# Attention with top-k and two expert layers: the first pair's preparation, the routing's instructions, the gathers' buffers and the fold table are rearranged

## The chip, the cores and the metric

One NeuronCore of a Trainium2 chip runs the whole program. The metric is the device time of one execution in microseconds (us); lower is better. The core has five engines with a queue of their own each, and they meet only through semaphores: TensorE (PE: matmuls and transposes through the array; its weight loads are listed as PEld), VectorE (DVE), ScalarE (ACT), GpSimd (POOL) and SyncE (SP), whose queue issues most of the DMAs. Matmul results land in PSUM, everything else lies in SBUF or in DRAM.

## What is computed

The reference has three stages, on 4 batches of 576 tokens with 8 heads of 64 columns (so 2304 tokens of 512 columns):

```python
# attention, for each batch and head
scores = scale * (q @ k.T)                                  # 576 x 576
kth = the 32nd largest of each row of scores
scores = where(scores >= kth, scores, -1e9)
attn = softmax(scores)                                      # with 1e-9 added to the sum
x[:, head] = attn @ v
# experts: one of 8 for each token that is not skipped
do_compute = x @ w_skip > 0
e_idx = argmax(x @ w_gate);  gate_w = softmax(x @ w_gate)[e_idx]
x[do_compute] += gate_w * (relu(x @ w1[e_idx]) @ w2[e_idx]) # 512 -> 1024 -> 512
# gated layer for all tokens
g = x @ w_gate2;  out = (g * sigmoid(g) * (x @ w_val)) @ w_out   # 512 -> 1536 -> 512
```

## The kernel before

The tokens are worked on in two groups of two batches (`NG`, `BG`). For each group: attention, routing, experts (`moe1`), gated layer (`moe2`).

**Attention** (`attention`, L333) goes through 16 pairs of heads (group, batch, pair), each with nine tiles of 128 query rows: four of the first head, one that holds the last 64 rows of both heads, four of the second (`SEQ`, L305). For each tile PE makes the scores (`scores`, L200), ACT copies them out (`head`, L212), and DVE finds the 32 largest of each row (`rows_tile`, L225): a maximum of the two halves (`hi`, L222 or L236), then rounds of MAX8 and MATCH_REPLACE8 (L241, L255, L256). POOL makes the minima in the first half (L252, L253) and the bias `nb` of the exponential (L243). In the first half (`whole(w)`: nine pairs) PE and ACT apply the mask; after that DVE does (L260). `trans` and `pv` (L272, L281) transpose the weights and multiply by v. The second step of `pv` (L301) multiplies the result by `fold`, a table for each head with an identity folded in two, the gate's 8 columns and the skip's one: so one product gives the 64 output columns and the head's share of the routing logits.

**Preparation of a pair** (`prep`, L112). q and k are needed with the head's columns on the partitions, and as two fp32r parts whose sum is the fp32 value. For each of the two heads (i) and for k, then q: the rows are loaded, the high part is copied and the low part subtracted into the tile `nat` (L149, one buffer), which `prep_t` (L178) transposes on PE into a bank of `side_bank` (one bank in the first half) and copies out on ACT. For the first pair (`first`) ACT makes the high parts (L154) and DVE the low ones (L160); for all others POOL makes both (L156, L159, L160). All loads are issued by SP. The first pair has nothing beside it; each later pair is prepared during the nine tiles of the one before.

**Routing** (`route`, L454, `first_slots`, L534) runs once for each group and batch, on five tiles of up to 128 tokens. DVE takes the largest of 8 logits, the index of the first that equals it and a one-hot row; PE counts the tokens ahead of each with triangular ones; DVE reads off the rank. `first_slots` then builds, with a one-hot of the rank (`hot`) and a product on PE, the list of the first 128 token rows of each expert, with the gate's weight (`ids`). Loops over the five tiles issue one small instruction for each (L478, L487, L521, L543). L527 to L532 compute a slot in a table of all tokens; only `tables` reads it, inside a branch (`rest`, L738) that runs when an expert has more than 128 tokens of a group or when a row has a tie at the 32nd place.

**Experts** of the first group (`moe1_whole`, L1058) run among the tiles of the second group's attention. For expert e, `gather` (L967) fetches its rows from DRAM into a tile `io` with an indirect DMA on POOL's queue, one expert ahead; `turn` transposes them (L1070); the two layers follow in fp32; DVE adds the gated result into the same tile (L1104), and `scatter` (L975) writes the rows back. `io` has two buffers (`nio`, the last argument of `Moe` at L657). `moe2` of that group uses the same tile to load its rows and to store its output. In between, `split_gated` (L563) converts and splits the gated layer's weights, on DVE (L611 to L613), ACT (L590) and POOL (L591).

**The order of the work.** The Python code writes the instructions in an order that interleaves these stages by counts of steps (`run`, L615; `ORDER`, L30). The tile framework then simulates the program and draws each engine's order from priorities and simulated times (`high_priority`, `issue_after` are hints to it), and puts in the semaphores. On the chip each engine runs its list strictly in that order.

## Time and profile before

| | us |
|---|---|
| median of 3 runs | 1231.78 |
| lowest and highest run | 1224.69, 1232.47 |
| the profiled execution | 1217.23 |
| its span, first to last instruction | 1215.4 |
| PE busy | 1158.9 |
| DVE busy | 976.2 |
| ACT busy | 733.4 |
| POOL busy | 592.2 |

The profile is one execution, with its own time. Times in the rows are microseconds from the first instruction of the span. An instruction counts as busy from its start to its end, waits inside it included; matmul ends are modelled. The entry in brackets at the end of a row is how long the engine was idle before it, and what released it.

### The profile page before, as it was taken

The numbers are of one execution on the slowest core, as the hardware profiler recorded it, in microseconds if no ns is written. First come the engines' busy times: TensorE is split into PE (matmuls) and PEld (weight loads), VectorE is DVE, ScalarE is ACT, GpSimd is POOL, SyncE is SP. The second block draws the span as 40 slices with busy tenths as digits, with TensorE's granted clock in tenths as the row PEclk, the third lists the DMA queues.
The fourth block names the chain that finished last, engine by engine and source line by source line (L and its number), as shares of the span: only waits on it lengthen the run. The fifth ranks groups of instructions, "written<-read, shape, count | busy, mean of one in ns | idle before, by whom it ended". The sixth has DMA issues, their size and how long they took to land.

```text
span 1215.4 us, 21497 instructions
## 1 busy us (share of the span) xinstructions
PE 1158.9 (95%) x7253; PEld 1002.6 (82%) x7254; DVE 976.2 (80%) x2366; ACT 733.4 (60%) x1582; POOL 592.2 (49%) x770
## 2 busy tenths in 40 slices
PE   6999889999899999999999999999999999999997
PEld 5777778777687877888887799899998799898996
DVE  6999999999999999999999982369888268184480
ACT  5989988999664565656555442267767344343440
POOL 6788867888243434335444433222111535555550
PEclk9999999999899999999998999999999999999999
DMA  2023621111178979876655786799888534543430
GB/s 70 22 79 122 204 66 40 39 36 35 62 248 279 322 256 323 293 252 214 210 189 208 258 298 218 267 342 296 293 269 289 189 101 124 171 125 119 150 102 29
DMA packets 136796, 219.11 MB, mean 180 GB/s; under 512 B 37860, under 2 KB 95204, under 8 KB 130404
## 3 DMA queue, kind: packets, MB, share of 16 engines
q1 hardware_dynamic: 129652, 178.86, 44.6%
q0 software_dynamic: 7024, 38.78, 9.3%
q8 instruction: 59, 0.97, 0.3%
q14 instruction: 61, 0.50, 0.1%
HBM read 177.77 MB, written 41.95 MB: 181 GB/s over the span
## 4 chain that ended last, share of the span: by engine, by line
PE 47%; DVE 19%; DMA 8%; issue 3%; ACT 3%; POOL 1%; SPq 0%; DVEq 0%; POOLq 0%; ACTq 0%
PE m L1155 7%; PE m L1156 7%; PE m L1157 7%; DVE tops L256 5%; DVE rest L255 5%; PE m L1179 4%; PE m L1180 4%; PE m L1178 4%; PE m L1101 2%; DVE pp L260 2%; PE pT L291 1%; DVE rest L248 1%; PE pT L277 1%; DMA h2h<-in_moe_w_out_dram 1%; DMA wraw<-in_moe_w_dram 1%
## 5 line engine op out<-in xcount | busy, mean ns | idle before, releaser
L256 DVE MAX8 tops<-rest 128x8 f32<-128x288 f32 (+1 forms) x432 | 229.2, 545 | 1.2
L1155 PE MATMUL m<-x2h,whl 128*128 128x384 f32 x576 | 196.0, 341 | 1.9 <-ACT x2h L1140 1.4
L1157 PE MATMUL m<-x2h,whl 128*128 128x384 f32 x576 | 194.0, 338 | 0.9 <-POOL whl L591 0.9
L1156 PE MATMUL m<-x2l,whl 128*128 128x384 f32 x576 | 194.6, 338 | 0.0
L1124 POOL TENSOR_TENSOR whl<-wfly,whl 128x1024 fp32r<-128x1024 f32 x54 | 129.5, 2399 | 111.6 <-ACT whl L1123 111.6
L1123 ACT ACTIVATE whl<-wfly 128x1024 fp32r<-128x1024 f32 x69 | 73.2, 1060 | 105.2 <-PE m L1157 65.5
L279 ACT ACTIVATE pt<-pT 128x512 f32<-128x512 f32 (+2 forms) x320 | 112.1, 405 | 37.4 <-PE pT L277 36.0
L255 DVE MATCH_REPLACE8 rest<-tops,rest 128x288 f32<-128x288 f32 x288 | 125.7, 437 | 0.0
L218 ACT ACTIVATE sc<-pS 128x576 f32<-128x576 f32 x144 | 93.6, 650 | 32.9 <-PE pS L208 24.9
L277 PE MATMUL pT<-idn,pp 128*128 128x128 f32 (+1 forms) x720 | 109.7, 278 | 3.0 <-DVE pp L260 1.0
L1155 PEld LDWEIGHTS m<-x2h,whl 128*128 128x128 f32 x576 | 108.0, 188 | 5.4 <-ACT x2h L1140 1.7
L1157 PEld LDWEIGHTS m<-x2h,whl 128*128 128x128 f32 x576 | 108.1, 188 | 1.4 <-POOL whl L591 1.3
L208 PE MATMUL pS<-kT,qT 128*128 128x288 f32 x512 | 105.4, 326 | 3.4 <-DVE hi L222 1.6
L1156 PEld LDWEIGHTS m<-x2l,whl 128*128 128x128 f32 x576 | 108.2, 188 | 0.5
L1167 DVE TENSOR_TENSOR h2l<-th,h2h 128x384 fp32r<-128x384 f32 x36 | 86.3, 2397 | 23.9 <-ACT h2h L1166 23.9
L960 DVE TENSOR_TENSOR whl<-wraw,whl 128x1024 fp32r<-128x1024 f32 x64 | 80.4, 1269 | 20.8 <-ACT whl L959 19.1
L1164 DVE SCALAR_TENSOR_TENSOR th<-th,m 128x384 f32<-128x384 f32 x72 | 39.1, 543 | 71.4 <-ACT th L1163 71.4
L243 POOL TENSOR_SCALAR nb<-tops 128x1 f32<-128x1 f32 x144 | 36.8, 255 | 121.9 <-DVE tops L241 101.3
L277 PEld LDWEIGHTS pT<-idn,pp 128*128 128x128 f32 (+1 forms) x720 | 80.7, 137 | 13.1 <-issue 6.4
L208 PEld LDWEIGHTS pS<-kT,qT 128*128 128x128 f32 x512 | 77.9, 196 | 9.9 <-ACT sc L218 2.8
L1178 PE MATMUL m<-whl,h2h 128*128 128x512 f32 x216 | 84.9, 398 | 0.5 <-DMA whl<-w2s 0.3
L1179 PE MATMUL m<-whl,h2h 128*128 128x512 f32 x216 | 85.2, 394 | 0.0
(205 smaller groups left out, 2913.9 us busy)
## 6 DMA issues: line engine op xcount, KB each, us to landing
wfly<-w2s SPq DMA_DIRECT2D x69, 512.0 KB, 3.5
whl<-in_moe_w_dram SPq DMA_DIRECT2D x32, 1024.0 KB, 6.2
wraw<-in_moe_w_dram SPq DMA_DIRECT2D x64, 512.0 KB, 5.4
whl<-w2s POOLq DMA_DIRECT2D x31, 1024.0 KB, 6.3
w2s<-h2h SPq DMA_DIRECT2D x8, 1024.0 KB, 8.8
w2s<-whl SPq DMA_DIRECT2D x8, 1024.0 KB, 9.3
io<-xa SPq DMA_DIRECT2D x18, 256.0 KB, 4.1
out_dram<-io SPq DMA_DIRECT2D x18, 256.0 KB, 2.1
```

Source lines behind the costliest of these rows:

```text
L208: m = self.nc.tensor.matmul(pS[:, x, :W], l, r[:, x * W:(x + 1) * W], start=(n == 0), stop=stop and n == len(ops) - 1)
L218: self.nc.scalar.activation(sc, pS[:, :, :W], AF.Copy, scale=BIG if on_pe else 1.0)
L255: self.mark = nc.vector.match_replace(hj, h[:, (j - 1) * 8:j * 8], hi if j == 1 else hj, NEG)
L256: nc.vector.max(h[:, j * 8:(j + 1) * 8], hj if j < 3 else rest.rearrange("p a b -> p (a b)"))
L277: self.anchor = nc.tensor.transpose(p[:k, c - a, :], pp[:, c * P:c * P + k], self.idn)
L279: nc.scalar.activation(T[:k, a:z, do:do + n], p[:k, :z - a, so:so + n], AF.Copy)
L1124: self.fly_engine.tensor_tensor(lo, raw, hi.bitcast(F32), op=OP.subtract)
L1155: nc.tensor.matmul(pz, wh[:, z, k, :], xh[:, k, :], start=(k == 0), stop=False)
L1156: nc.tensor.matmul(pz, wh[:, z, k, :], xl[:, k, :], start=False, stop=False)
L1157: nc.tensor.matmul(pz, wl[:, z, k, :], xh[:, k, :], start=False, stop=(k == 3))
L1178: nc.tensor.matmul(po[t], hh[:, f, s], wh[:, k, :], start=(f == 0), stop=False)
L1179: nc.tensor.matmul(po[t], hh[:, f, s], wl[:, k, :], start=False, stop=False)
```

## The change

- `fold` has one entry for two heads: the identity stands once, with the even head's nine weight columns ahead of it and the odd head's behind it. `pv` takes the 73 columns that it needs from either side; so an even head's output now stands behind its logits (`finish_pair` reads it there). POOL makes 4 instead of 8 identities, and eight smaller loads replace four.
- First pair, first head only (`lead`): q's two loads of this head go out on ACT's queue; q's `nat` lies in a pool of its own (`tmp`); the transposes go to `pt_bank`, three banks instead of one; DVE takes the copies of k's tail and of q's second half. The first pair's second head is prepared as all others are, on POOL.
- Routing: the loops over five tiles become single instructions over all five (L479, L488, L522, L544). The table of column numbers becomes bf16.
- The slot arithmetic moves into a new function `slots`, called from `tables`, with tiles kept for each group and batch (`routed`).
- `io` of the first group's experts gets three buffers.

```diff
@@ -43 @@
         self.rps = None
-        self.L, self.ids = {}, {}
+        self.L, self.ids, self.routed = {}, {}, {}
         self.const = ctx.enter_context(tc.tile_pool(name="const", bufs=1))
@@ -64 @@
         E, D, H = self.E, self.D, self.H
-        self.fold = c.tile([P, H, D + E + 1], F32, name="fold")
-        for h in range(H):
-            nc.gpsimd.tensor_tensor(self.fold[:, h, :D], self.idn[:, :D], self.idn[:, D:], op=OP.add)
+        M = E + 1
+        self.fold = c.tile([P, H // 2, D + 2 * M], F32, name="fold")
+        for j in range(H // 2):
+            nc.gpsimd.tensor_tensor(self.fold[:, j, M:M + D], self.idn[:, :D], self.idn[:, D:], op=OP.add)
...
         self.before = c.tile([P, P], BF, name="before")
-        self.column = c.tile([P, P], F32, name="column")
+        self.column = c.tile([P, P], BF, name="column")
         nc.gpsimd.iota(self.column, pattern=[[1, P]], base=0, channel_multiplier=0,
@@ -83 @@
                        allow_small_or_imprecise_dtypes=True)
-        self.ebase = c.tile([P, 5, E], F32, name="ebase")
-        nc.gpsimd.iota(self.ebase, pattern=[[0, 5], [self.GT, E]], base=0, channel_multiplier=0,
-                       allow_small_or_imprecise_dtypes=True)
         self.rows = c.tile([P, NT, 1], I32, name="rows")
...
             f = self.fold[x * D:(x + 1) * D]
-            nc.sync.dma_start(f[:, :, D:D + E], self.a["moe_w_gate"].rearrange("(h p) e -> p h e", p=D))
-            nc.sync.dma_start(f[:, :, D + E], self.a["moe_w_skip"].rearrange("(h p) -> p h", p=D))
+            for hh, o in ((0, 0), (1, D + E + 1)):
+                nc.sync.dma_start(f[:, :, o:o + E],
+                                  self.a["moe_w_gate"].rearrange("(h z p) e -> z p h e", z=2, p=D)[hh])
+                nc.sync.dma_start(f[:, :, o + E], self.a["moe_w_skip"].rearrange("(h z p) -> z p h", z=2, p=D)[hh])
         self.nblk = c.tile([1, self.NG * E], I32, name="nblk")
@@ -116 @@
         def load(nm, t, i, parts=(0, 1)):
-            src, eng = self.a[nm], nc.sync
+            src = self.a[nm]
+            eng = nc.scalar if first and i == 0 and nm == "q" else nc.sync
             o = src.offset + (b * self.H + h + i) * S * D
@@ -146 @@
                 n = 5 - i
-                t = sb.tile([P, 5, 3 * D], F32R, name="nat", bufs=1)
+                lead = first and i == 0
+                t = (self.tmp if lead and nm == "q" else sb).tile([P, 5, 3 * D], F32R, name="nat", bufs=1)
                 o = t[:, :n, :w * D].rearrange("p c (t e) -> p c t e", t=w)
                 src = raws[nm][:, i, :n, :]
-                if first:
+                if lead:
                     for z in range(0, w, 2):
@@ -157 @@
                     nc.gpsimd.tensor_scalar(o[:, :, 0, :], src, 1.0, 1.0, op0=OP.mult, op1=OP.mult)
-                (nc.vector if first else nc.gpsimd).tensor_tensor(o[:, :, 1, :], src, o[:, :, 0, :].bitcast(F32),
+                (nc.vector if lead else nc.gpsimd).tensor_tensor(o[:, :, 1, :], src, o[:, :, 0, :].bitcast(F32),
                                                                   op=OP.subtract)
-                nat = (nm, i, t, kT, qT, qt)
+                nat = (nm, i, t, kT, qT, qt, lead)
                 yield
@@ -175 @@
-    def prep_t(self, nm, i, t, kT, qT, qt):
+    def prep_t(self, nm, i, t, kT, qT, qt, lead):
         nc, D = self.nc, self.D
+        bank = self.pt_bank if lead else self.side_bank
+        def copy(o, p, alt):
+            if lead and alt:
+                nc.vector.tensor_copy(o, p)
+            else:
+                nc.scalar.activation(o, p, AF.Copy)
         nz = 1 if nm == "k" else 2
         for z in range(nz):
-            p = self.side_bank(F32R)
+            p = bank(F32R)
             for c in range(4):
                 nc.tensor.transpose(p[:, c, :], t[:, c, D * z:D * z + P], self.idr)
-            nc.scalar.activation(kT[i][:, :512] if nm == "k" else qT[i][:, z, :],
-                                 p.bitcast(F32).rearrange("p c e -> p (c e)"), AF.Copy)
+            copy(kT[i][:, :512] if nm == "k" else qT[i][:, z, :], p.bitcast(F32).rearrange("p c e -> p (c e)"),
+                 nm == "q" and z == 1)
         if i:
             return
-        p = self.side_bank(F32R)
+        p = bank(F32R)
         for z in range(nz):
...
             if nm == "k":
-                nc.scalar.activation(kT[j][:, 512:], pf[:, 0, s], AF.Copy)
+                copy(kT[j][:, 512:], pf[:, 0, s], True)
             else:
@@ -284 @@
         M = D + self.E + 1
+        fold = self.fold[:, h // 2, :M] if h % 2 == 0 else self.fold[:, h // 2, M - D:]
         v = R["v"]
@@ -298 @@
         for j, (so, n, dst) in enumerate(outs):
-            nc.tensor.matmul(p[:n, j, :M], oT[:, so:so + n], self.fold[:, h], start=True, stop=True)
+            nc.tensor.matmul(p[:n, j, :M], oT[:, so:so + n], fold, start=True, stop=True)
         for j, (so, n, dst) in enumerate(outs):
@@ -432 @@
             cols = slice(j * P + hh * D, j * P + (hh + 1) * D)
-            nc.sync.dma_start(d[b * S:b * S + 512, cols].rearrange("(p c) d -> p c d", c=4), x[:, :4, hh, :D])
-            nc.sync.dma_start(d[b * S + 512:(b + 1) * S, cols], x[:64, 4, hh, :D])
+            nc.sync.dma_start(d[b * S:b * S + 512, cols].rearrange("(p c) d -> p c d", c=4), x[:, :4, hh, M - D if hh == 0 else 0:][:, :, :D])
+            nc.sync.dma_start(d[b * S + 512:(b + 1) * S, cols], x[:64, 4, hh, M - D if hh == 0 else 0:][:, :D])
         yield
...
             for hh in range(2):
-                nc.gpsimd.tensor_tensor(l, l, x[:n, s, hh, D:], op=OP.add)
+                nc.gpsimd.tensor_tensor(l, l, x[:n, s, hh, D * hh:][:, :, :M - D], op=OP.add)
         if j == H // 2 - 1:
@@ -467 @@
         nc.vector.tensor_reduce(m, lg, axis=AX.X, op=OP.max)
-        do = t2("do")
+        if (g, b) not in self.routed:
+            self.routed[g, b] = (c.tile([P, NT, E], BF, name=f"oh{g}{b}"), c.tile([P, NT], F32, name=f"sl{g}{b}"),
+                                 c.tile([P, NT], F32, name=f"do{g}{b}"))
+        oh, sl, do = self.routed[g, b]
+        if every:
+            do = t2("do")
         nc.vector.tensor_scalar(do, L[:, :, E], 0.0, None, op0=OP.is_gt)
...
         if every:
-            do = t2("all")
+            do = self.routed[g, b][2]
             nc.vector.memset(do, 1.0)
...
         eq = t3("eq")
-        for t in range(NT):
-            nc.vector.scalar_tensor_tensor(eq[:, t], lg[:, t], m[:, t:t + 1], self.erow[:, t], op0=OP.is_equal,
-                                           op1=OP.mult)
+        def wide(x):
+            return x[:, :, None].to_broadcast([P, NT, E])
+        nc.vector.tensor_tensor(eq, lg, wide(m), op=OP.is_equal)
+        nc.vector.tensor_tensor(eq, eq, self.erow, op=OP.mult)
         d = t3("d")
-        nc.vector.tensor_tensor(d, lg, m[:, :, None].to_broadcast([P, NT, E]), op=OP.subtract)
+        nc.vector.tensor_tensor(d, lg, wide(m), op=OP.subtract)
         nc.scalar.activation(d, d, AF.Exp)
...
         nc.vector.tensor_reduce(idx, eq, axis=AX.X, op=OP.min)
-        oh = t3("oh", BF)
-        for t in range(NT):
-            nc.vector.scalar_tensor_tensor(oh[:, t], self.erow[:, t], idx[:, t:t + 1],
-                                           do[:, t:t + 1].to_broadcast([P, E]), op0=OP.is_equal, op1=OP.mult)
+        nc.vector.tensor_tensor(eq, self.erow, wide(idx), op=OP.is_equal)
+        nc.vector.tensor_tensor(oh, eq, wide(do), op=OP.mult)
         yield
@@ -517 @@
         yield
-        rk, sl = t3("rk"), t2("sl")
-        for t in range(NT):
-            nc.vector.scalar_tensor_tensor(rk[:, t], pk[:, t * E:(t + 1) * E], 1.0, oh[:, t], op0=OP.mult, op1=OP.mult,
-                                           accum_out=sl[:, t:t + 1])
+        rk = t3("rk")
+        nc.vector.tensor_tensor(rk, pk[:, :NT * E].rearrange("p (t e) -> p t e", t=NT), oh, op=OP.mult)
+        nc.vector.tensor_reduce(sl, rk, axis=AX.X, op=OP.add)
         if not every:
...
         nc.vector.tensor_copy(data[:, :, 0:1], rows)
-        ns = t2("ns")
+    def slots(self, g, b):
+        nc, c, NT, E = self.nc, self.const, 5, self.E
+        oh, sl, do = self.routed[g, b]
+        ns = c.tile([P, NT], F32, name="r_ns")
+        rk = c.tile([P, NT, E], F32, name="r_rk")
+        idx = c.tile([P, NT], F32, name="r_idx")
         nc.vector.tensor_scalar(ns, do, -1.0, -1.0e6, op0=OP.add, op1=OP.mult)
@@ -540 @@
         hot = self.at.tile([P, 5, P], F32, name="hot")
-        for t in range(5):
-            nc.vector.tensor_scalar(hot[:, t], self.column, rank[:, t:t + 1], None, op0=OP.is_equal)
+        nc.vector.tensor_tensor(hot, self.column[:, None, :].to_broadcast([P, 5, P]),
+                                rank[:, :, None].to_broadcast([P, 5, P]), op=OP.is_equal)
         yield
@@ -627 @@
             with ExitStack() as s1:
-                tmp = self.pool(s1, "tmp")
+                tmp = self.tmp = self.pool(s1, "tmp")
                 self.at1 = self.pool(s1, "attn1")
@@ -654 @@
                     pass
-            mo = Moe(self, self.pool(st, "moe"), self.psum_pool(st, "pm"), 3, ring, 2)
+            mo = Moe(self, self.pool(st, "moe"), self.psum_pool(st, "pm"), 3, ring, 3)
             mo.ready = ready
@@ -758 @@
         sent = sb.tile([P, n, 2], I32, name="sent")
+        self.ebase = sb.tile([P, 5, self.E], F32, name="ebase")
+        nc.gpsimd.iota(self.ebase, pattern=[[0, 5], [self.GT, self.E]], base=0, channel_multiplier=0,
+                       allow_small_or_imprecise_dtypes=True)
         nc.gpsimd.iota(sent[:, :, 0], pattern=[[0, n]], base=self.GT, channel_multiplier=0)
...
             nc.sync.dma_start(tab.rearrange("(p n) c -> p (n c)", p=P), sent.rearrange("p n c -> p (n c)"))
+            for b in range(self.BG):
+                self.slots(g, b)
             for t in range(self.NT):
...
```

## Rows read from the trace of the kernel before

**Rows 1.** Windows: microseconds busy of each engine in three stretches (start:end, length)

```profile
13.00:315.00 302.00, 282.96 (x2125) 231.19 (x2125) 301.15 (x971) 269.35 (x705) 234.74 (x391) 0.99 0.24 72
315.00:700.00 385.00, 367.15 (x2275) 304.05 (x2274) 372.56 (x999) 218.87 (x511) 159.74 (x226) 0.98 0.71 243
...
760.00:1215.00 455.00, 443.57 (x2483) 407.92 (x2482) 268.00 (x305) 218.31 (x307) 171.27 (x92) 0.99 0.58 191
```

**Rows 2.** Timeline of the start: start, length, engine, line, operation [idle before, releaser]

```profile
1.22 1.22 SPq L130 DMA_DIRECT2D raw<-in_k_dram  x2
...
3.10 1.10 SPq L130 DMA_DIRECT2D raw<-in_q_dram  x2
...
3.89 0.47 ACT L154 ACTIVATE nat<-raw 128x320 fp32r<-128x320 f32 x1 [1.21 <-DMA raw<-in_k_dram]
...
4.98 0.75 PE L184 MATMUL pR<-idr,nat 128*128 128x128 f32 x4 [4.98 <-DVE nat L160]
...
6.41 0.37 PE L191 MATMUL pR<-idr,nat 128*128 128x128 f32 x1 [0.69 <-ACT kT L185]
...
7.04 0.83 ACT L154 ACTIVATE nat<-raw 128x320 fp32r<-128x320 f32 x2
...
7.54 0.49 DVE L160 TENSOR_TENSOR nat<-raw,nat 128x320 fp32r<-128x320 f32 x1 [2.35 <-ACT nat L154]
...
8.87 0.60 ACT L185 ACTIVATE qT<-pR 128x512 fp32r<-128x512 f32 x1 [1.01 <-PE pR L184]
...
11.52 0.85 PE L208 MATMUL pS<-kT,qT 128*128 128x288 f32 x2
...
12.41 0.65 ACT L218 ACTIVATE sc<-pS 128x576 f32<-128x576 f32 x1 [0.94 <-PE pS L208]
...
13.09 0.46 DVE L236 TENSOR_TENSOR hi<-sc 128x288 f32<-128x288 f32 x1 [5.06 <-ACT sc L218]
...
13.14 1.07 POOL L252 TENSOR_TENSOR sm<-sc 128x288 int32<-128x288 int32 x1 [6.38 <-ACT sc L218]
```

**Rows 3.** The tile nat in the first 30 us: durations in ns, min/median/max

```profile
L160 DVE TENSOR_TENSOR nat<-raw,nat x4: 491/529/735, 4.4 to 16.9; 128x320 fp32r<-128x320 f32 x2, 128x256 fp32r<-128x256 f32 x2
...
L160 POOL TENSOR_TENSOR nat<-raw,nat x2: 876/877/878, 23.9 to 28.2; 128x320 fp32r<-128x320 f32 x2
```

**Rows 4.** DVE by lines, 166 to 187 us (one routing): count, us, mean ns, idle

```profile
L488 DVE SCALAR_TENSOR_TENSOR r_oh<-erow,r_idx,r_do 128x8 bf16<-128x8 f32 x5 | 1.3, 314 | 0.0
L544 DVE TENSOR_SCALAR hot<-column,r_sl 128x128 f32<-128x128 f32 x5 | 1.1, 274 | 0.0
...
L479 DVE SCALAR_TENSOR_TENSOR r_eq<-L,r_m,erow 128x8 f32<-128x8 f32 x5 | 0.8, 212 | 0.0
L528 DVE TENSOR_SCALAR r_ns<-r_do 128x5 f32<-128x5 f32 x1 | 0.7, 679 | 0.0
...
L522 DVE SCALAR_TENSOR_TENSOR r_rk<-pR,r_oh 128x8 f32<-128x8 f32 x5 | 0.5, 145 | 0.0
...
L482 DVE TENSOR_TENSOR r_d<-L,r_m 128x40 f32<-128x40 f32 x1 | 0.2, 183 | 0.0
```

**Rows 5.** Timeline behind two of the gathers

```profile
372.15 1.04 POOL L969 DMA_INDIRECT io<-xa,ids  x1 [3.35 <-DMA xa<-io,ids]
...
376.55 0.63 PE L1070 MATMUL m<-idn,io 128*128 128x128 f32 x4 [2.40 <-DMA io<-xa,ids]
...
378.45 0.46 DVE L222 TENSOR_TENSOR hi<-sc,pS 128x288 f32<-128x288 f32 x1 [1.80 <-ACT sc L218]
...
408.04 0.46 DVE L222 TENSOR_TENSOR hi<-sc,pS 128x288 f32<-128x288 f32 x1 [1.06 <-ACT sc L218]
```

**Rows 6.** Waits of POOL's engine over the run: us in total, times, longest

```profile
POOL io L969 <- DMA xa<-io,ids: 10.2, 5, 3.7
```

**Rows 7.** Timeline at 347 us, DVE and POOL

```profile
347.19 2.35 POOL L591 TENSOR_TENSOR h2h<-h2h 128x1024 fp32r<-128x1024 f32 x1
...
347.73 2.43 DVE L260 SCALAR_TENSOR_TENSOR pp<-sc,tops,e 128x576 f32<-128x576 f32 x1
```

## The prediction

> **What bounds the kernel now.** I read the busy time by stretch first, because the averages of the page mix stages with different limits [rows 1]. From 13 to 315 us VectorE (DVE) is busy 301.15 of 302.00 us, while TensorE (PE) has 19 us idle: the first half of the attention is set by DVE, and every DVE microsecond taken out of it moves all that follows. From 315 to 700 us, where attention, the first group's experts and the weight splitting share the core, DVE is busy 372.56 of 385.00 and PE 367.15: DVE still leads, with 12.4 us of idle time, but PE is close behind. From 760 on PE is busy 443.57 of 455.00 and DVE 268.00; there time taken from DVE is worth nothing, and work that starts earlier simply ends earlier.
>
> Then I read the timeline of the start [rows 2]. DVE's first attention instruction starts at 13.09, after 5.06 us idle, and until then the engines take turns on one chain: k is split (ACT, then DVE), transposed (PE), copied out (ACT), and only then q is split, because k and q share one buffer of the tile `nat`, and one PSUM bank. Next come the DVE instructions of one routing [rows 3, 4], and last what the experts' gathers wait for [rows 5, 6].
>
> **The change part by part.**
>
> *First pair side by side.* Both ends of the chain stay; the middle is run in parallel. k is unchanged up to its transposes, which end at 4.98 + 0.75 = 5.73. q's two loads of the first head leave from ACT's queue, which at the start has only the table load and one copy to do; the last piece of q (the second head's 64-row tail) is SP's fourth issue: k's tails are issued by 1.22 + 1.22 = 2.44, one issue costs half of 1.10, so 2.99. k's last tail was issued by 2.44 and ACT took k at 3.89, 1.45 later; so q is there at about 4.45. ACT copies it by 4.45 + 0.83 = 5.28, DVE subtracts by 5.8 (0.49). PE does k's tail by 5.73 + 0.37 = 6.10, q's first half by 6.85 and the second by 7.6 (0.75 each). With three banks no copy blocks them, and the second half's copy goes to DVE, which idles there; the trace has no such copy on DVE, so I take ACT's 0.60 for it and get 8.2. Scores: first half 6.85 + 0.60 + 0.85 = 8.3, second half to 9.15, eviction 0.65: DVE starts at about 9.9 instead of 13.09. A gain of **3.1**. Bounds: if ACT issues the two loads only behind its first copy, q comes some 1.5 later and 1.6 is left; if they also hold back ACT's copy of k (two issues of 0.55), 0.5; 3.6 at best.
>
> *The second head's splits on POOL.* Two DVE subtractions at 529 ns [rows 3] leave the stage that DVE bounds: **1.0** gained. On POOL they cost two at up to 0.88 plus two copies, say 3.0 us. What hides them: POOL idles 6.38 us before its first attention instruction at 13.14 [rows 2], and half of its eight fold additions go as well. If that cover is gone, POOL's part of the first tile is up to 3 us late; DVE then has the next tiles' maxima to do, so the bounds are -1.3 and 1.3.
>
> *Routing on five tiles at once.* Per routing, from one of the four [rows 4]: L488 1.3, L479 0.8, L544 1.1, L522 0.5 and L528 0.7 go, with four small ones behind L528 (0.5 in all, none over L482's 0.18): 4.9 us. In come five instructions of 128x40 and one reduction of the same size, 6 x 0.18 = 1.1, and one comparison of 128x640: from 0.18 at 40 elements and 0.46 at 288 (the first `hi` in rows 2) 1.13 ns each, so 0.18 + 600 x 1.13 ns = 0.86. Net 3.0. Without the stretched rows (L528 at 0.2, L488 at L479's 0.8) it is 2.0. I take 2.5, between them. Three routings lie in the stage that DVE sets (168, 303, 528 us): **7.5**, bounds 6.0 and 9.0. The fourth, at 773, is where PE is the bound: nothing. The slot arithmetic goes into a branch of which the trace shows no instruction.
>
> The merged comparison is the one place where a rule speaks against the edit. The Trainium skill ("VectorE: DVE Perf Modes", section on the TRN2 errata) gives 58 + elements/speed-up cycles, with a speed-up of 2 for an fp32 tensor_scalar out of SBUF and none for tensor_tensor: an estimate by that page is 5 x 122 cycles = 0.64 us before and 698 cycles = 0.73 after, a loss of 0.1 where the rows give a gain of 0.24. By the page the sum would be 1.0 lower.
>
> *Three row blocks.* With two, the gather for expert e+1 must wait until the scatter of e-1 has landed, since it writes into that block. POOL waits 10.2 us for this over five gathers [rows 6], and what stands behind on its queue waits too: at 372.15 the gather starts after 3.35 us idle, the bias `nb` of a softmax tile comes behind it, PE sits 2.40 us before the transposes of the gathered rows, and DVE idles 1.80 until 378.45 [rows 5]. The same ends in 1.06 us at 408.04. With a third block the gather waits for a scatter one expert older, long landed. I count the two that DVE shows: **2.9**, bounds 0 and 8 (most of DVE's 12.4 idle there). What is late next is the scatter's own wait for its expert's result.
>
> *Nothing.* The shared fold table: the multiplication keeps its 73 columns. Its eight loads instead of four add four SP issues, about 2.5 us of SP's queue at 10 to 15 us, ahead of the next pair's loads; the next pair's splits are needed some 30 us later. If that cover failed, it would be up to 2.5.
>
> Sum: 3.1 + 1.0 + 7.5 + 2.9 = 14.5. The profiled execution took 1217.23 us (span 1215.4), so 1202.7 by its measure. The median of the runs shown stands 14.55 higher, at 1231.78; from it, **1217.3**.
>
> **The rivals.**
>
> A. *The second half gives nothing.* PE is 95% busy there, and a stall taken from one engine may only be handed to the next. For it: PE's 367.15 of 385. Against: the gap at 378 runs through both. The third routing and the gathers fall away: 14.5 - 2.5 - 2.9 = 9.1, 1222.7.
>
> B. *The wide instructions are held by POOL.* At 347.73 a DVE instruction with two SBUF inputs takes 2.43 us beside a POOL subtraction of 2.35 that started just before [rows 7]. Five of the new wide instructions have two SBUF inputs, the merged comparison among them, where its five predecessors had one tensor input. If each is held for half of a POOL instruction of 1.07 (the one at 13.14), a routing gains nothing: 5 x 0.5 = 2.5. Then 14.5 - 7.5 = 7.0, 1224.8. Against: the old L488 and L479 had two inputs as well, and more instructions to be caught. The Trainium skill ("SBUF — State Buffer", section "Who interferes with whom") states it as a rule: a VectorE instruction with two SBUF inputs and a GpSimd instruction that reads SBUF exclude each other for a whole instruction. By that rule, the pair at 347 agrees.
>
> C. *The gather's wait moves into PE's queue: slower.* The order on each engine is drawn at build from simulated times. With the third block the transposes of gathered rows may be put earlier among the scores than the data really lands; PE works in order, so scores, and then DVE, wait behind them. Place: L1070, eight experts. Price: DVE idled 1.80 for PE's 2.40, three quarters. Without the gathers' 2.9 the change gains 11.6; it turns into a loss from a wait of 11.6 / 0.75 / 8 = 1.9 us per expert. At POOL's present 3.35 it is 20.1 - 11.6 = 8.5 lost, 1240.3. Against: a gather issued sooner also lands sooner.
>
> D. *The second half closes up.* If all of DVE's 12.4 us idle goes instead of 2.9, the gain is 24.0, 1207.8. For it: the bias behind a waiting POOL is a common end of the gaps there. Against: most of them are shorter than a microsecond and end with other things.
>
> **How the numbers follow.** Chances: my forecast 0.52 (its own range 1211 to 1223, from the bounds of the four terms taken in moderate mixture), A 0.16, B 0.12, D 0.12, C 0.08. The range 1203 to 1229 takes in A, B and D, with D's end stretched by 5 for the spread of the runs (the quickest of before stands 7.1 under the median) and the upper end by the low bounds of all terms; it leaves out C and tails. A measurement of this kernel tells about 1% from no change, here 12.3 us, so faster means under 1219.5: 0.7 of my forecast, D and a little of A, 0.54. Slower is C, 0.07. The rest, 0.39, is within.
>
> **What would show it.** Right: the first `hi` near 10 us; about 2.5 us less DVE time in each routing; L969 no longer waiting for a landing; DVE's busy time down by some 9 to 11 us (the fourth routing included), its stage ending near 685 instead of 700. Wrong: a first `hi` after 11.5; the merged comparison over 1.2 us; new idle time before L1070; or DVE's idle time from 315 on grown by more than the start has won.

## The result, and the profile after

The kernel after takes **1213.74 us** (median of 12 runs, 1209.92 to 1218.01). The kernel before takes 1224.58 in the 12 runs beside it (1216.64 to 1232.47). The ratio is 0.9914, with a 95% interval of 0.9890 to 0.9939: some 10.5 us quicker. 1217.3 was predicted, with a drop of 14.5 us.

The profiled execution after took 1210.6 us, with a span of 1208.7: 6.7 under the span of before, whose profiled execution is one of its quicker ones. Both profiles can be accounted for on PE, which is busy 96% of the span: after, its idle time is 52.1 us against 56.5 of before (1.8 less until 13 us, 0.8 less until 315, 1.1 less until 760, 0.8 less behind it), and its busy time is 2.3 less. No single place gives the gain. The last routing starts at 773.0 before and at 774.0 after, so the 6.7 us lie behind it: PE does 5.9 us less from 760 us on (443.57 and 437.64), as it stood still 3.7 less until then, and its busy time is 2.3 less in all.

The windows of the kernel after, columns as in [rows 1]:

```profile
13.00:315.00 302.00, 283.71 (x2120) 229.00 (x2119) 299.38 (x941) 268.58 (x702) 232.19 (x389) 0.99 0.24 72
315.00:700.00 385.00, 368.24 (x2277) 306.57 (x2275) 365.26 (x947) 217.86 (x503) 162.04 (x225) 0.98 0.75 251
760.00:1208.00 448.00, 437.64 (x2461) 399.89 (x2458) 264.31 (x280) 215.51 (x303) 174.88 (x90) 1.00 0.60 192
```

DVE has lost 7.3 us of work between 315 and 700 us, but has not closed up: it idles 19.7 us there, where it idled 12.4. PE's busy time is 1.1 higher. The attention, which was to end near 685 us, ends *later* than before (the last MAX8 of a `hi` by 6 us); it is the other work of that stretch (the first group's experts, the weight splitting) that is 4 to 10 us earlier.

The start of the kernel after, as in [rows 2]:

```profile
0.77 0.41 ACTq L123 DMA_DIRECT2D raw<-in_q_dram  x1
...
1.22 0.56 ACTq L131 DMA_DIRECT2D raw<-in_q_dram  x1
...
1.80 1.28 ACT L63 ACT_TABLE_LOAD   x1 [1.68 <-issue]
...
4.16 1.45 ACT L156 ACTIVATE nat<-raw 128x320 fp32r<-128x320 f32 x3 [0.75 <-DMA raw<-in_k_dram]
...
5.21 0.75 PE L194 MATMUL pT<-idr,nat 128*128 128x128 f32 x4 [5.21 <-DVE nat L162]
...
7.38 0.69 DVE L186 CAST qT<-pT 128x512 fp32r<-128x512 f32 x1 [0.90 <-PE pT L194]
...
8.00 0.68 PE L218 MATMUL pM<-kT,qT 128*128 128x288 f32 x2
...
8.48 0.67 PE L194 MATMUL pR<-idr,nat 128*128 128x128 f32 x4
...
8.94 0.81 PE L218 MATMUL pS<-kT,qT 128*128 128x288 f32 x2
...
9.79 0.65 ACT L228 ACTIVATE sc<-pS 128x576 f32<-128x576 f32 x1
...
10.47 0.57 DVE L246 TENSOR_TENSOR hi<-sc 128x288 f32<-128x288 f32 x1 [2.40 <-ACT sc L228]
```

The first `hi` starts at 10.47 instead of 13.09: 2.6 us won. ACT's two issues push its table load to 1.80, and the copy of k comes at 4.16 instead of 3.89.

DVE's lines in the first routing of the kernel after, columns as in [rows 4]:

```profile
L566 DVE TENSOR_TENSOR hot<-column,sl 128x640 f32<-128x640 bf16 x1 | 1.3, 1342 | 0.0
...
L487 DVE TENSOR_SCALAR do<-L 128x5 f32<-128x5 f32 x1 | 0.8, 830 | 0.0
...
L499 DVE TENSOR_TENSOR r_eq<-r_eq,erow 128x40 f32<-128x40 f32 x1 | 0.3, 348 | 0.0
...
L506 DVE TENSOR_TENSOR oh<-r_eq,do 128x40 bf16<-128x40 f32 x1 | 0.2, 186 | 0.0
...
L498 DVE TENSOR_TENSOR r_eq<-L,r_m 128x40 f32<-128x40 f32 x1 | 0.2, 180 | 0.0
```

The new wide instructions take 0.18 to 0.35 us here (up to 0.54 in the second routing), the merged comparison 1.34 here and about 0.8 in the other three. With every DVE instruction of a routing counted from the end of the one before it, the four routings took 6.67, 6.88, 5.23 and 5.16 us before, and take 3.87, 3.05, 2.84 and 3.23 after. The merged comparison of 1.34 starts just behind an instruction on POOL:

```profile
183.03 0.79 POOL L263 TENSOR_TENSOR rest<-sm,hi 128x288 int32<-128x288 int32 x1 [1.54 <-DVE tops L266]
183.17 1.34 DVE L566 TENSOR_TENSOR hot<-column,sl 128x640 f32<-128x640 bf16 x1
```

The gathers (L997) and scatters (L1004) of the first group in the kernel after, on POOL's timeline, and POOL's wait for them over the run, against [rows 5, 6]:

```profile
323.78 1.89 POOL L997 DMA_INDIRECT io<-xa,ids  x1 [1.40 <-DVE rest L265]
325.96 0.97 POOL L997 DMA_INDIRECT io<-xa,ids  x1 [0.30 <-issue]
327.24 0.95 POOL L997 DMA_INDIRECT io<-xa,ids  x1 [0.30 <-issue]
361.23 1.08 POOL L1004 DMA_INDIRECT xa<-io,ids  x1 [7.62 <-DVE io L1132]
367.78 1.17 POOL L997 DMA_INDIRECT io<-xa,ids  x1 [5.47 <-DMA xa<-io,ids]
```

```profile
POOL io L997 <- DMA xa<-io,ids: 15.9, 4, 5.5
```

Three gathers are issued ahead instead of two, so no PE instruction waits for gathered rows any more (three waited 3.9 us before). But four of the five later gathers still come right behind the scatter that frees their block, and POOL still waits for that landing: 15.9 us, where it was 10.2.

### The profile page after: what moved, and what is told of

The parts are those of the page before. It is cut to its first block, busy times and chain, and to the rows that moved or that the text cites. A ratio compares the mean times of both kernels' runs of the same rounds, so it can differ in the third digit from the quotient of the medians.

```text
span 1208.7 us, 21428 instructions
## 1 busy us (share of the span) xinstructions
PE 1156.7 (96%) x7253; PEld 997.0 (82%) x7254; DVE 969.1 (80%) x2275; ACT 731.2 (60%) x1576; POOL 600.7 (50%) x769
## 4 chain that ended last, share of the span: by engine, by line
PE 46%; DMA 10%; DVE 10%; ACT 3%; issue 2%; POOL 1%; SPq 0%; DVEq 0%; ACTq 0%; POOLq 0%
PE m L1183 6%; PE m L1184 6%; PE m L1185 6%; PE m L1207 4%; PE m L1208 4%; PE m L1206 4%; DMA wraw<-in_moe_w_dram 4%; PE m L1116 3%; DVE whl L988 2%; DMA w2s<-h2h 2%; PE m L1129 2%; PE pT L302 2%; PE pS L218 2%; PE pT L287 2%; DVE tops L266 1%
## 5 line engine op out<-in xcount | busy, mean ns | idle before, releaser
L287 PE MATMUL pT<-idn,pp 128*128 128x128 f32 (+1 forms) x720 | 113.2, 278 | 0.3 <-DVE pp L270 0.3
L218 PE MATMUL pS<-kT,qT 128*128 128x288 f32 x512 | 101.8, 321 | 4.9 <-DVE hi L232 2.7
L987 ACT ACTIVATE whl<-wraw 128x1024 fp32r<-128x1024 f32 x64 | 67.2, 1061 | 33.1 <-DMA wraw<-in_moe_w_dram 24.4
L1206 PE MATMUL m<-whl,h2h 128*128 128x512 f32 x216 | 85.9, 401 | 0.6 <-DVE x2l L1169 0.6
L1195 POOL TENSOR_TENSOR h2l<-th,h2h 128x384 fp32r<-128x384 f32 x36 | 46.2, 1283 | 80.7 <-ACT h2h L1194 80.6
```

Of the source, the lines that this page charges most:

```text
L218: m = self.nc.tensor.matmul(pS[:, x, :W], l, r[:, x * W:(x + 1) * W], start=(n == 0), stop=stop and n == len(ops) - 1)
L287: self.anchor = nc.tensor.transpose(p[:k, c - a, :], pp[:, c * P:c * P + k], self.idn)
L1195: lo_engine.tensor_tensor(hl[:, f, :], th, hh[:, f, :].bitcast(F32), op=OP.subtract)
L1206: nc.tensor.matmul(po[t], hh[:, f, s], wh[:, k, :], start=(f == 0), stop=False)
```

## The experiments

The change has three parts that can be made alone, so these came first, with the kernel before run again as its own control.

**lead_only**: the first pair side by side (with the second head's splits on POOL), nothing else.

```diff
-            src, eng = self.a[nm], nc.sync
+            eng = nc.scalar if first and i == 0 and nm == "q" else nc.sync
...
-                t = sb.tile([P, 5, 3 * D], F32R, name="nat", bufs=1)
+                t = (self.tmp if lead and nm == "q" else sb).tile([P, 5, 3 * D], F32R, name="nat", bufs=1)
...
-                (nc.vector if first else nc.gpsimd).tensor_tensor(o[:, :, 1, :], src,
+                (nc.vector if lead else nc.gpsimd).tensor_tensor(o[:, :, 1, :], src,
...
-            p = self.side_bank(F32R)
+            p = bank(F32R)
```

> Only the first pair is changed: q's loads on ACT's queue, its own nat tile, three banks, two copies on DVE, and the second head's splits on POOL; routing, row blocks and fold table as before. If my terms stand and add, the first hi is at 10.5 us as in the changed kernel and the run is 4.1 us quicker than before (ratio 0.9967, within 0.9950 to 0.9985). The rival: the start is won and given back, because ACT, PE and POOL cannot keep DVE fed behind it; then the ninth tile is under 1 us early and the ratio is 0.999 to 1.001.

**route_only**: the routing on five tiles at once, with the slot arithmetic moved and `column` in bf16.

```diff
-        for t in range(NT):
-            nc.vector.scalar_tensor_tensor(eq[:, t], lg[:, t], m[:, t:t + 1], self.erow[:, t], ...)
+        nc.vector.tensor_tensor(eq, lg, wide(m), op=OP.is_equal)
+        nc.vector.tensor_tensor(eq, eq, self.erow, op=OP.mult)
...
-        for t in range(5):
-            nc.vector.tensor_scalar(hot[:, t], self.column, rank[:, t:t + 1], None, op0=OP.is_equal)
+        nc.vector.tensor_tensor(hot, self.column[...], rank[...], op=OP.is_equal)
```

> Only the routing is changed: wide instructions and the slot arithmetic moved into the branch. If DVE sets the time up to 700 us, three routings give 2.5 each: 7.5 us, ratio 0.9939. If the second half (from 315 us) gives nothing, two routings count: 5.0 us, ratio 0.9959. If POOL holds the wide instructions, the merged comparison is above 1.2 us in each routing and the ratio is above 0.998.

**blocks_only**: three row blocks and the shared fold table that makes room for the third.

```diff
-        self.fold = c.tile([P, H, D + E + 1], F32, name="fold")
+        self.fold = c.tile([P, H // 2, D + 2 * M], F32, name="fold")
...
-            mo = Moe(self, self.pool(st, "moe"), self.psum_pool(st, "pm"), 3, ring, 2)
+            mo = Moe(self, self.pool(st, "moe"), self.psum_pool(st, "pm"), 3, ring, 3)
```

> Only the third row block, with the shared fold table that makes room for it. If the gathers' wait cost what DVE showed, 2.9 us are won (ratio 0.9976) and POOL's wait of 10.2 us before L969 is gone. The rival: the stall is handed on and the second half is filled by PE anyway; then the wait is gone, the attention's last tile is not earlier, and the ratio is 0.999 to 1.002.

**same_again**: the kernel before with no edit, run as if it were another.

> The kernel before, unchanged, for its spread and the granted clock of each of its runs. Its runs lie between 1216 and 1232 us, those of the changed kernel between 1210 and 1218. If the spread is the time that the clock takes, span times granted clock is the same in all runs to about 2 us, and part of the gain of the median (10.8 us, against 6.7 between the quickest runs) is fewer stretches at the lower clock. If it is something else, span times clock spreads as the span does. Ratio 1.000 within 0.002 either way.

Measured, as ratios to the kernel before: lead_only **1.0093** (1.0063 to 1.0122), route_only **0.9906** (0.9873 to 0.9938), blocks_only 0.9987 (0.9963 to 1.0012), same_again 1.0005 (0.9973 to 1.0037). The routing alone gives the whole gain. The lead alone makes the kernel 11 us *slower*, although its start is won as in the kernel after. The three don't add up: 11.4 - 11.5 - 1.6 is -1.7, and together they give -10.5. For blocks_only, POOL's wait for landings is 7.2 us in two waits, not gone. For same_again, the spread is mostly not the clock's: its twelve spans lie 14.5 us apart, and span times granted clock still 12.4.

Where lead_only loses, its timeline at 375 us, where [rows 5] show the kernel before at the same work:

```profile
374.66 1.03 POOL L979 DMA_INDIRECT io<-xa,ids  x1 [6.08 <-DMA xa<-io,ids]
375.72 2.36 POOL L601 TENSOR_TENSOR h2h<-h2h 128x1024 fp32r<-128x1024 f32 x1
378.03 0.20 POOL L253 TENSOR_SCALAR nb<-tops 128x1 f32<-128x1 f32 x1
...
378.27 0.77 ACT L257 ACTIVATE e<-sc,nb 128x576 f32<-128x576 f32 x1 [7.01 <-POOL nb L253]
...
379.42 1.56 PE L311 MATMUL pT<-fold,oT 128*128 128x73 f32 x6 [5.48 <-ACT oT L307]
...
380.57 0.46 DVE L232 TENSOR_TENSOR hi<-sc,pS 128x288 f32<-128x288 f32 x1 [5.54 <-ACT sc L228]
```

The gather waits 6.08 us on POOL; the bias `nb` stands behind it and a weight subtraction; ACT waits 7.01 for the bias, PE 5.48 for ACT, DVE 5.54 for the scores. The same gather cost DVE 1.80 in the kernel before: what differs is what the build has put behind it. For the order of the instructions on each engine is drawn anew at every build, from times that it works out itself. Compared engine by engine, lead_only keeps only some half of PE's instructions of the second half in the places that they have in the kernel before.

And the stall is paid for twice. The windows of lead_only around it:

```profile
374.00:379.00 5.00, 0.00 (x0) 0.00 (x0) 1.03 (x4) 0.73 (x2) 3.72 (x4) 1.00 0.50 181
379.00:385.80 6.80, 6.38 (x21) 5.28 (x22) 3.23 (x10) 3.85 (x11) 1.47 (x5) 0.50 0.49 174
385.80:395.00 9.20, 9.20 (x52) 7.82 (x50) 8.37 (x22) 2.83 (x5) 1.44 (x2) 1.00 0.86 285
```

PE does nothing for 5 us; for the next 6.8 us the granted clock is 0.50, the lower of its two levels.

This stall is not the whole of the loss. From 315 to 760 us PE idles 30.8 us in lead_only and 17.9 in the kernel before, and 5.5 of the 12.9 between them lie here. And route_only, among the quickest, has a stall much like it, with 6.8 us at the lower clock:

```profile
364.95 1.00 POOL L983 DMA_INDIRECT io<-xa,ids  x1 [5.68 <-DMA xa<-io,ids]
...
371.04 1.09 PE L1084 MATMUL m<-idn,io 128*128 128x128 f32 x4 [5.16 <-DMA io<-xa,ids]
```

```profile
369.20:376.00 6.80, 4.96 (x14) 3.57 (x14) 3.53 (x11) 2.23 (x4) 0.41 (x2) 0.50 0.60 224
```

Two theories were then open: the lead costs by what it contains (a third issuing queue, other banks, POOL's splits), or through the order alone. Two kernels tell them apart, each with 0.45 us of double copying on ACT in the start of the kernel *before* and no edit of the change. Doubled for k, the build keeps the order of the kernel before; doubled for q, it draws that of lead_only (99% and more of the instructions in the same place behind the first eighth).

**copy_k_twice** and **copy_q_twice**, the second with "q" for "k":

```diff
-                    for z in range(0, w, 2):
+                    for z in [0] * (i == 0 and nm == "k") + list(range(0, w, 2)):
```

> The kernel before with one piece of work doubled: the first pair's high copy of the first two token tiles of k (ACT, about 0.45 us) is made twice, with the same result. Its engines' order is that of the kernel before, in all parts. Theory 'the order decides': the chain of the start is longer by at most 0.5 us and the rest follows it; ratio 0.999 to 1.002, the same second half from 315 us on with its gaps of 1.8 and 1.1 us on DVE. Theory 'the content of the lead costs': the same here, at most 0.5 us.

> The kernel before with the same 0.45 us of double copying, on q instead of k. None of the lead's edits is in it, but the build draws for it the order of lead_only on PE, DVE and POOL (99 to 100% of the instructions in the same place behind the first eighth). Theory 'the order decides': it loses what lead_only lost or a little more, since it has the long start as well: 11 to 15 us over before, ratio 1.009 to 1.013, with the gap of some 5.5 us on DVE near 380 us behind the gather and the bias. Theory 'the content of the lead costs' (its third queue, its banks, the second head's splits on POOL): within 0.5 us of before, ratio 0.998 to 1.002.

Measured: copy_k_twice 1.0009 (0.9985 to 1.0034), copy_q_twice **1.0108** (1.0077 to 1.0139). None of the lead's edits is in it, and it loses what lead_only loses. lead_only and copy_q_twice also lose it in step: counted at the same `hi` of the attention, they stand level with and 3.4 us behind the kernel before at 326 us, 8.6 and 8.9 behind at 449, and 13.8 and 14.2 behind at 697 (same_again, without any edit, stands 3.4 behind there). One part of the expectation missed: near 380 us DVE idles 1.93, not 5.5. There its time goes in another way:

```profile
375.32 1.03 POOL L969 DMA_INDIRECT io<-xa,ids  x1 [3.84 <-DMA xa<-io,ids]
...
376.38 2.35 POOL L591 TENSOR_TENSOR h2h<-h2h 128x1024 fp32r<-128x1024 f32 x1
...
376.65 2.70 DVE L260 SCALAR_TENSOR_TENSOR pp<-sc,tops,e 128x576 f32<-128x576 f32 x1
...
378.70 0.70 POOL L243 TENSOR_SCALAR nb<-tops 128x1 f32<-128x1 f32 x1
...
379.44 0.77 ACT L247 ACTIVATE e<-sc,nb 128x576 f32<-128x576 f32 x1 [5.30 <-POOL nb L243]
...
381.74 0.45 DVE L222 TENSOR_TENSOR hi<-sc,pS 128x288 f32<-128x288 f32 x1 [1.93 <-ACT sc L218]
```

`pp`, with two inputs out of SBUF, takes 2.70 us beside a POOL subtraction (the pattern of [rows 7]); its median is 0.81.

Next, two parts were taken out of the kernel after.

**without_blocks**:

```diff
-            mo = Moe(self, self.pool(st, "moe"), self.psum_pool(st, "pm"), 3, ring, 3)
+            mo = Moe(self, self.pool(st, "moe"), self.psum_pool(st, "pm"), 3, ring, 2)
```

> The kernel after with two row blocks instead of three, all else kept. Theory 'the third block is worth the wait that it removes': between 2.9 us (the two DVE gaps of before) and 6 (the gap of lead_only besides): ratio to before 0.994 to 0.996. Theory 'the order decides': the second half is drawn anew from PE's instruction 1989 on and can come out anywhere between 0.988 and 1.003. Theory 'the third block is worth nothing': 0.991, as the kernel after.

**without_lead**: the diff of lead_only, taken back in the kernel after.

> The kernel after with the first pair as before (k, then q, one buffer, all splits on DVE and ACT). The second half of the order is mostly that of the kernel after (but not at 480 to 600 us). Theory 'the start's 2.6 us reach the end': ratio to before 0.993 to 0.994. Theory 'the start's gain is given back by 150 us, and the lead acts through the order alone': 0.989 to 0.992 where the order stays good. Theory 'the lead costs by its content': 0.980 to 0.984, since the lead alone was 11 us slower.

Measured: without_blocks 0.9897 (0.9865 to 0.9928), without_lead 0.9898 (0.9868 to 0.9927). Neither part is worth anything that can be measured beside the routing, in the orders that were drawn. Yet the third block does remove a wait. The timeline of without_blocks:

```profile
363.15 1.00 POOL L997 DMA_INDIRECT io<-xa,ids  x1 [5.46 <-DMA xa<-io,ids]
...
371.71 1.09 PE L1098 MATMUL m<-idn,io 128*128 128x128 f32 x4 [6.25 <-DMA io<-xa,ids]
...
377.23 0.82 DVE L270 SCALAR_TENSOR_TENSOR pp<-sc,tops,e 128x576 f32<-128x576 f32 x1 [6.29 <-PE pT L287]
```

PE idles 6.25 us before gathered rows and DVE 6.29, a gap that the kernel after doesn't have. Over 315 to 760 us PE idles 18.3 us here and 16.8 in the kernel after: of a wait of 6.25 taken away, 1.5 is left in the sum.

Last, the routing: is its gain its DVE time, or a good draw? Adding DVE time redraws the order too, so the same computation was padded twice by different amounts, beside two more draws without the routing.

**routing_padded** and **hot_twice**, in the kernel after, with 4 and with 2:

```diff
-        nc.vector.tensor_tensor(hot, ...)
+        for _ in range(4):
+            nc.vector.tensor_tensor(hot, ...)
```

> The kernel after with the merged comparison made four times instead of once (same result): three more instructions of 1.26, 0.72 and 0.73 us in the routings at 168, 303 and 528 us, 8.1 us of DVE time, which nearly gives back the 9.1 us that the routing on five tiles saves there. The rest of the routing stays. Theory 'the routing's DVE time is the gain': ratio to before 0.996 to 1.000. Theory 'the routing's gain is its order, or the shorter waits between its steps': 0.989 to 0.993, as the kernel after. The order of the middle is drawn anew too, so that a value over 1.004 would mean a poor draw and tell neither.

> The same with the merged comparison made twice: 2.7 us of DVE time given back in the three routings, and another draw of the order (48 to 80% of the instructions between 165 and 700 us stay in their place against the kernel after). Theory 'the routing's DVE time': 0.992 to 0.994, about a third of the way to routing_padded. Theory 'order': anywhere between 0.988 and 1.003, and not between the two others.

**copy_k1_twice**: the edit of copy_k_twice, with `i == 1` for `i == 0`. That is the second head of the first pair, where the text below says the second pair.

> The kernel before with the second pair's copy of k's first two token tiles made twice (some 0.45 us on ACT, beside 30 us of time until it is needed). It takes part in nothing that this change touches, but the build draws another order from there on (from PE's instruction 76; 38 to 82% kept in the stretch that ends at 700 us). Theory 'the order decides': a ratio off 1 by more than the 0.1% that the work is worth, either way, anywhere from 0.992 to 1.011. Theory 'only content counts': 0.998 to 1.002.

**without_routing**: the diff of route_only, taken back in the kernel after.

> The kernel after with the old routing: first pair side by side, three row blocks and shared fold table. The first quarter of the order is that of lead_only, from PE's instruction 1993 on it is drawn anew, most like blocks_only. Parts added up (lead_only 1.0093, blocks_only 0.9987): 1.008. Theory 'the routing brings all of it, lead and blocks nothing': 0.998 to 1.002, above the kernels with the routing by 0.8% or more. My prediction's terms (3.1 + 1.0 + 2.9 us): 0.994.

Measured: routing_padded 0.9991 (0.9967 to 1.0015), hot_twice 1.0036 (1.0011 to 1.0061), copy_k1_twice 1.0071 (1.0046 to 1.0096), without_routing 1.0102 (1.0067 to 1.0136). In the traces the extra comparisons take 6.6 us in three routings of routing_padded and 2.2 in hot_twice, not the 8.1 and 2.7 expected: the repeats take 0.72 to 0.74 each, in the first routing too, where 1.26 had been counted. The loss of routing_padded fits the theory of DVE time in its sign: 6.6 us given back cost 9.4 (0.9991 less 0.9914, of 1222.4). hot_twice contradicts it: 2.2 us given back cost 15. And the padding costs more than DVE time. In routing_padded:

```profile
339.55 1.12 PE L1099 MATMUL m<-idn,io 128*128 128x128 f32 x4 [6.38 <-DMA io<-xa,ids]
...
342.81 0.45 DVE L232 TENSOR_TENSOR hi<-sc,pS 128x288 f32<-128x288 f32 x1 [2.68 <-ACT sc L228]
```

Its second routing ends 10 us later than in the kernel after (332.8 and 322.8 us), the first gather starts at 335.67 instead of 323.78, and PE stands before the gathered rows; hot_twice waits there for 3.20. A repeated copy of 0.42 us (copy_k1_twice), 0.3 us of delay at the `hi` of 39.5 us, costs 0.7%. So a draw by itself moves this kernel by up to 1%, as much as the whole change, and between two kernels of different order a term of this size can't be weighed.

All kernels side by side, with the mean granted clock over the timed runs of each, and PE's busy time from 315 to 760 us in its profile:

| kernel | ratio | clock | PE busy, us |
|---|---|---|---|
| before, same_again | 1, 1.0005 | 0.987, 0.986 | 427.2, 426.3 |
| copy_k_twice (same order) | 1.0009 | 0.987 | 423.3 |
| blocks_only | 0.9987 | 0.987 | 425.8 |
| copy_k1_twice | 1.0071 | 0.987 | 425.1 |
| lead_only, copy_q_twice (one order) | 1.0093, 1.0108 | 0.983, 0.983 | 414.3, 417.0 |
| without_routing (lead and blocks) | 1.0102 | 0.979 | 414.6 |
| after, without_lead (nearly one order) | 0.9914, 0.9898 | 0.989, 0.992 | 428.2, 431.3 |
| route_only, without_blocks (one order) | 0.9906, 0.9897 | 0.991, 0.988 | 426.2, 426.7 |
| hot_twice, routing_padded | 1.0036, 0.9991 | 0.986, 0.985 | 419.0, 421.2 |

The four kernels with the routing and without padding are two draws, not four. Behind the first eighth, route_only and without_blocks have all of PE's instructions in the same place, and after and without_lead have 87% (after and route_only 52%). So route_only and without_blocks, which differ by the lead and the fold table, compare them at one order: 0.9906 and 0.9897, a difference of 1.1 us, well inside their intervals. By its content the lead does not cost 11 us.

## Why the prediction was right, and where it was not

The size came out within its own range (1211 to 1223): faster, by 10.5 us instead of 14.5. Part of that is luck. 1217.3 was counted from 1231.78, the median of three runs, and twelve runs put the kernel before at 1224.58: a base 7.2 too high and a drop 4.0 too large cancel in part. And of the four terms one carried it; the sum was right by that alone.

**The routing, 7.5 predicted: supported, not settled.** In the three routings of the stage that DVE sets, the DVE time fell by 2.8, 3.8 and 2.4, 9.0 together, the upper bound; alone it made the kernel 11.5 us faster. In the first half, where DVE is full, it can be followed: between the `hi` at 159.7 and the one at 310.6 us the kernel after gains 2.9 us on the kernel before, route_only 2.9, without_blocks 2.0, without_lead 1.2, the padded ones 1.3 and 0.9, and none of the kernels without the routing gains any. All four kernels with the routing and without padding lie at 0.990 or 0.991, all kernels without it at 0.9987 or above. That the gain comes with the routing is shown for the orders drawn. That it does so by its DVE time is supported by those 1 to 3 us of the first half and by routing_padded, and not settled: the order of the attention's instructions differs there too, part may be a better draw, and hot_twice, with the routing too, came out at 1.0036. The merged comparison took about 0.8 us, as estimated (0.86), and 1.34 once. The Trainium skill ("VectorE: DVE Perf Modes", the TRN2 errata) priced it at 0.73, close to that; but it priced the five single ones at 0.64, where the trace has 1.1. They take 0.196 us each behind the one before, as if the speed-up of 2 had not come about: without it the same row gives 0.97 for five, an estimate. On the loss that it would make, the measurement decides: 0.3 us less in three routings of four.

**First pair, 3.1 predicted: mis-sized, then given back.** The first `hi` came 2.6 us earlier. ACT's two issues did hold its copy of k up by 0.27, but that was made good: the copy of q's second half ended at 8.07, where I had 8.2. The half microsecond is lost behind it. I had PE go from the first half of the scores straight to the second, which was to end at 9.15; PE makes the product for `pM` and the second head's transposes in between (8.00 to 9.15), and the second half ends at 9.75. What I had not seen is that a lead at the start has to last. Counted at the same `hi` the kernel after is 2.7 us ahead at 36 us, 1.1 at 68 and 0.5 at 149; DVE idles 1.01 us before a `hi` at 29.90, which waits for its scores, and some `hi` of 0.57 us and more stand where 0.46 is usual. The step "every DVE microsecond taken out of it moves all that follows" failed for this term: that DVE is full does not make it wait for nothing once it is ahead. without_lead, and the pair of one order above, show that no more than about 1 us of it can reach the end. The second head's splits on POOL are part of the lead, and were not run by themselves.

**Three row blocks, 2.9 predicted: nothing.** The step "with a third block the gather waits for a scatter one expert older, long landed" is wrong: the third block is used up by a third gather ahead, and four of the five later ones still wait for the scatter just issued (15.9 us on POOL for 10.2). What went is PE's wait for the rows. It was worth 0.0013 of the time alone, inside its interval, and nothing that shows in the kernel after; both comparisons change the order too, so a small worth cannot be excluded.

**The fold table, nothing predicted:** blocks_only contains it and is at 0.9987, so no cost shows.

**The rivals.** A's drop (9.1) lies nearer to the 10.5 measured than my 14.5, and the closing up that it denies did not come about: DVE's idle time from 315 to 700 us grew by 7.3, the sign that I had named for "wrong". But 4.1 of its 9.1 were the lead, which gave next to nothing, so A's sum is not shown either. B (POOL holds the wide instructions) is seen in one merged comparison of four, and does not decide. C (the gather's wait in PE's queue) did not come about in the kernel after, where no PE instruction waits for gathered rows; with the same three blocks it did in the padded ones (6.38 and 3.20 us). D did not come about. And a loss of C's size exists: it came with the lead, through the order, and the two orders drawn with the routing and no padding are free of it. No rival of mine had the redrawn order itself as its mechanism, with a price of up to 1% of either sign; that is what the range should have named.

## What to carry to other kernels

Where the build orders the engines' instructions itself, a change is its own content and a new draw: make the edit alone, and beside it an edit of no content that draws the same order and one that keeps the old. Believe a part only when it holds over several draws, and count kernels of one order as one. Waits removed from one engine of a stretch in which three are nearly full come back elsewhere (6.25 us became 1.5), while work removed from the engine that sets the pace showed in both draws that were not padded.

## What the runs showed of the hardware that was not expected

A pause of PE can cost more than itself. In lead_only 5 us without a matmul are followed by 6.8 us at a granted clock of 0.50, and the three kernels in which PE is busy least from 315 to 760 us (414 to 417) have the lowest mean clock (0.979 to 0.983), the one with the most (without_lead, 431.3) the highest (0.992).

A DVE instruction with two SBUF inputs can be held through more than one POOL instruction. `pp`, 0.81 us in the median, took up to 2.43 us in the kernel before, 3.32 in hot_twice and 5.14 in copy_q_twice, there beside seven POOL instructions in a row, the first of 2.39:

```profile
639.29 2.39 POOL L591 TENSOR_TENSOR whl<-one,whl 128x1024 fp32r<-128x1024 f32 x1
...
640.40 5.14 DVE L260 SCALAR_TENSOR_TENSOR pp<-sc,tops,e 128x576 f32<-128x576 f32 x1
```

It does not decide the kernel's time: in sum over its 63 instructions `pp` takes 59.8 us before, 66.6 in copy_q_twice, 55.0 in routing_padded and 67.9 in the kernel after. The Trainium skill ("SBUF — State Buffer", "Who interferes with whom") calls the port that the two share an exclusive lock; the 2.70 us beside a subtraction of 2.35 agree.
